# A fused linear-attention and mixture-of-adapters kernel on one core: a new hand-written order, earlier last loads, a longer gate ahead of the stores, head-by-head sums in the last two batches

## The chip, the cores and the metric

The kernel runs on one core of one Trainium2 chip. The metric is device microseconds of one execution. A core has TensorE (PE in the profile), VectorE (DVE), ScalarE (ACT), GpSimd (POOL) and SyncE (SP); each runs its own list of instructions strictly in order, and semaphores between them hold an instruction back until what it needs is there. Sixteen DMA engines move data between HBM and SBUF.

## The reference, cut to what matters

Shapes: q, k and v are (8 batches, 8 heads, 576 positions, 64), float32; the output is (4608, 512).

```python
def phi(x, c, s):                       # c, s: cos and sin of pi/2 * pos / 576
    r = np.maximum(x, 0.0)
    return np.concatenate([r * c, r * s], axis=-1)
q_p = phi(q, cos_w, sin_w); k_p = phi(k, cos_w, sin_w)
kv = np.einsum('bhsf,bhsd->bhfd', k_p, v)          # sums over positions
z  = np.sum(k_p, axis=2)
num = np.einsum('bhsf,bhfd->bhsd', q_p, kv)
den = np.einsum('bhsf,bhf->bhs', q_p, z)[..., None] + 1e-06
x = (num / den) -> rows of 8 heads * 64 = 512
logits = x @ w_gate                                 # 8 experts, the best 2 count
w = softmax of the best 2 logits
out = x + sum over the 2 experts of w * (x @ A[e]) @ B[e]   # rank 16
```

## The kernel before, in words

**Order.** Everything is unrolled. The text `ORDER` (line 21) is one list of jobs, written out by hand: a name, an engine letter (T TensorE, A ScalarE, V VectorE, G GpSimd, S SyncE; W is GpSimd too) and indices. The program issues the jobs in this order, so the order of a letter's jobs is the order of that engine's queue. A job marked W also waits until the last VectorE job of the kinds `vs`, `rk` or `qc` ahead of it in the list has ended (line 493, reason "port").

**Per batch b.** `ldv`, `ldk`, `ldq` (lines 199 to 210) load v, k and q, 1152 KB of float32 each, which all but the first v and k are turned into bf16 by the DMA on its way; these 22 loads are issued by GpSimd and land one after the other. `vs` (line 240) multiplies v by the cos or sin table: 18 jobs of 128x256 a batch, spread over ScalarE, VectorE and GpSimd. `rk` (line 246) is the relu of k, `qc` (line 277) that of q, in two halves of 128x1152. `kv` (line 253), in three parts, lets TensorE sum k times (v, 1) over the positions into the PSUM tile `big`. `kve` (line 271) copies the sums to SBUF as bf16, in two jobs of 64 partitions, each into its own block of a tile whose other blocks stay zero (`kz`, line 264, sets them once), so that one matmul serves two heads.

**Per step n.** The 4608 tokens are 36 steps of 128 tokens, 4.5 steps a batch; step 4 of each nine takes 64 tokens of two batches ("mixed"). In a step: `qt` (line 284) transposes q, `qe` (line 292, VectorE) multiplies by the cos and sin tables, `nd` (line 299) does the matmuls for numerators and denominators, `re` and `no` (lines 332, 335, VectorE) divide, `xt` (line 346) transposes x, `xe` (line 351) copies it out of PSUM, `za` (line 355) multiplies by A and w_gate, `mx` (line 361, VectorE) finds the best logits. From step 27 on (`ROWS`), but not in the mixed step 31, `nd` uses 64-row matmuls, one head each. In each `nd`, the k-th division of the trace (`xt<-nd`) is that of step k.

**Per group of three steps.** VectorE does `nm` (sum of the best two logits, line 366), `mk`, `tt`, `cb`, ScalarE `sg` (sigmoid), VectorE `zg`; TensorE `zt` and a copy `ze` turn the result. Then, per step, `dx` (line 427) adds x and the adapters' part in one of the PSUM banks b0 and b1 (the two halves of `big`, which `kv` also uses) or q0 and q1; `oe` (line 442) copies the result to an output tile (22 of them, most laid over the loads of the first batches), and `st` (line 446) stores it, 256 KB.

**Gate.** SyncE's queue holds the first loads, then `gate` (line 219), then the 36 stores. `gate` is two tiny DMAs: the first reads a word of the last v and so waits for its load, the second reads what the first wrote and so waits for that one to land. Every store is queued behind.

Of the kernel before, what the change touches and what calls it, by code (L numbers as in the profile page):

```python
# [15 lines left out]
HALF = 64  # L16
# [5 lines left out]
ldv,S,0,0 pre,G start,A ldk,S,0,0 ldw,S ldq,G,0,0 tq,A ldv,G,1,0 ldk,G,1,0 ldq,G,1,0 ldv,G,2,0 vs,A,0,3,0  # L22
vs,V,0,5,1 ldk,G,2,0 cols,V vs,A,0,4,1 vs,V,0,7,1 vs,A,0,5,0 kz,G,1 kz,V,2 vs,A,0,8,0 vs,A,0,8,1 vs,A,0,1,0
vs,V,0,4,0 vs,A,0,7,0 kz,V,0 vs,A,0,0,1 vs,A,0,2,1 vs,A,0,0,0 vs,V,0,6,0 vs,A,0,1,1 vs,A,0,3,1 rk,V,0,0 rk,A,0,1
vs,V,0,2,0 vs,V,0,6,1 kv,T,0,0 qc,V,0,1 kv,T,0,1 qc,V,0,0 kv,T,0,2 qt,T,1 kve,A,0,0 qt,T,0 kve,A,0,1 qe,V,0
cw,A,0 qe,V,1 dm,T,n0 dm,T,n0 dm,T,n0 nd,T,0 qt,T,3 re,V,0 qt,T,2 no,V,0 qe,V,3 vs,G,1,8,0 vs,A,1,3,1 dm,T,b0
dm,T,b0 nd,T,1 vs,A,1,5,0 vs,G,1,6,1 vs,V,1,2,0 xt,T,0 vs,A,1,6,0 vs,W,1,7,1 xe,A,0 re,V,1 qe,V,2 vs,G,1,5,1
vs,A,1,8,1 vs,G,1,0,1 no,V,1 vs,A,1,2,1 ldq,G,2,0 vs,A,1,4,1 vs,V,1,1,1 dm,T,b0 dm,T,b0 dm,T,b0 dm,T,b0 dm,T,b0
dm,T,b0 nd,T,2 vs,V,1,1,0 vs,A,1,0,0 rk,V,1,0 ldv,G,3,0 xt,T,1 vs,A,1,7,0 xe,A,1 vs,V,1,4,0 ldk,G,3,0 dm,T,b0
kv,T,1,0 vs,V,1,3,0 re,V,2 za,T,0 no,V,2 ldq,G,3,0 kv,T,1,1 mx,V,0 nd,T,3 qc,V,1,0 xt,T,2 kv,T,1,2 re,V,3  # L30
qc,V,1,1 xe,A,2 za,T,1 no,V,3 kve,A,1,1 qt,T,4 qt,T,5 kve,A,1,0 za,T,2 qe,V,4 xt,T,3 mx,V,1 xe,A,3 mx,V,2 nd,T,4
# [5 lines left out]
vs,A,2,8,1 qc,V,2,0 xt,T,6 mk,V,1 kv,T,2,1 nm,V,1 re,V,7 xe,A,6 tt,V,1 cb,V,1 no,V,7 kv,T,2,2 sg,A,1 qt,T,9
zg,V,1 kve,A,2,0 nd,T,8 vs,W,3,0,1 qe,V,9 kve,A,2,1 vs,G,3,0,0 xt,T,7 zt,T,1 qt,T,10 vs,G,3,5,0 re,V,8 za,T,6
ze,A,1 no,V,8 qt,T,11 vs,G,3,5,1 xe,A,7 dx,T,2,b0 qe,V,10 vs,G,3,1,1 nd,T,9 oe,A,2 vs,G,3,2,1 qe,V,11 xt,T,8
vs,A,3,2,0 vs,G,3,8,1 za,T,7 dx,T,3,b1 re,V,9 xe,A,8 ldq,G,5,0 mx,V,7 no,V,9 dx,T,4,b0 vs,A,3,1,0 za,T,8  # L40
rk,V,3,0 vs,G,3,6,1 nd,T,10 oe,A,4 oe,A,3 xt,T,9 mx,V,6 mx,V,8 qt,T,12 re,V,10 vs,W,3,4,1 nm,V,2 vs,A,3,3,0
# [12 lines left out]
zt,T,4 no,V,17 vs,G,5,7,1 za,T,15 dx,T,11,b0 xe,A,16 vs,G,5,3,0 mx,V,15 qe,V,19 nd,T,18 ze,A,4 vs,G,5,4,0
# [56 lines left out]
def kernel(ctx, tc, q, k, v, w_gate, A, Bw, out):  # L111
# [107 lines left out]
    def gate(e, b):  # L219

        e.dma_start(out=gone, in_=v_b[b][0:1, 0, 0, 0:2])
        e.dma_start(out=gone2, in_=gone)
# [301 lines left out]
```

## Time and profile before

| | |
|---|---|
| runs shown | 105.68, 105.83, 105.94 us; median 105.83 |
| profiled execution, whole | 105.92 us |
| its span (first to last thing recorded) | 104.1 us |
| TensorE clock granted | 0.997 |

The span is 1.8 us shorter than the execution's own time; what lies around it is taken to be the same for both kernels. Sections 1 and 2 of the profile tell how full each engine is and when; the chain of waits tells which work ended last; the timeline gives single instructions: start, duration, engine, line, output, input, and in brackets the idle time before it and what ended that.

### The profile page before, as it was taken

To read this page: it belongs to the slowest core of one execution; us is meant where nothing else is said; L and a number is where in the kernel's file an instruction comes from. 1 tells how busy PE (TensorE), PEld (TensorE's weight loads), DVE (VectorE), ACT (ScalarE), POOL (GpSimd) and SP (SyncE) were. 2 spreads that over 40 slices of the span, in tenths; PEclk is the share of its full clock that TensorE was granted. 3 is DMA by queue.
4 is the path that set the end of the run, shared out by engine and by line. 5 is a ranking of instruction groups with operands and counts; after the bars stand their busy time and mean duration, and the time that the engine had idled before them with its cause. 6 is when DMAs were issued, how large, how long until landed. Compare 5 with 4: busy or idle time off the path is not lost.

```text
span 104.1 us, 3984 instructions
## 1 busy us (share of the span) xinstructions
PE 91.0 (87%) x1620; PEld 65.7 (63%) x1620; DVE 87.3 (84%) x264; ACT 82.3 (79%) x176; POOL 57.3 (55%) x112
## 2 busy tenths in 40 slices
PE   4999489879794999999999999999999999998810
PEld 1344267457573887867887789688778677665200
DVE  5058769579995999999999999999999999999710
ACT  6969767918899699999899789979984896967820
POOL 6991004960799696997979869998910000000000
PEclk9999999999999999999999999999999999999998
DMA  2999999999999999999999999999999996989992
GB/s 27 364 358 291 216 208 247 208 207 213 203 208 213 204 206 210 208 213 204 208 210 205 208 207 207 210 206 126 188 397 372 349 334 257 376 307 383 381 384 96
DMA packets 19225, 25.55 MB, mean 245 GB/s; under 512 B 2184, under 2 KB 13448, under 8 KB 19208
## 3 DMA queue, kind: packets, MB, share of 16 engines
q0 software_dynamic: 11616, 12.98, 73.8%
q1 hardware_dynamic: 7064, 12.21, 32.8%
q8 instruction: 12, 0.20, 0.7%
q10 hardware_dynamic: 528, 0.13, 0.6%
q14 instruction: 5, 0.04, 0.1%
HBM read 28.85 MB, written 9.44 MB: 368 GB/s over the span
## 4 chain that ended last, share of the span: by engine, by line
PE 53%; DMA 18%; ACT 11%; POOL 9%; issue 2%; DVE 2%; POOLq 0%; ACTq 0%
DMA q<-in_q_dram 18%; PE nd L324 10%; PE big L258 8%; PE xz L349 6%; PE za L358 6%; PE big L439 6%; PE big L440 5%; PE pq L289 5%; POOL vs L244 4%; ACT xT L353 3%; ACT zgT L423 2%; PE nd L313 2%; POOL q L200 2%; PE xz L415 2%; POOL k L200 1%
## 5 line engine op out<-in xcount | busy, mean ns | idle before, releaser
L244 POOL TENSOR_SCALAR vs<-v,tab 128x256 bf16<-128x256 bf16 x78 | 37.9, 501 | 17.8 <-DMA v<-in_v_dram 8.7
L353 ACT COPY xT<-xz 128x512 bf16<-128x512 bf16 x34 | 20.0, 587 | 8.9 <-PE xz L349 8.3
L297 DVE TENSOR_TENSOR qT<-pq,tabq 128x1024 bf16<-128x1024 bf16 x36 | 23.8, 676 | 0.9 <-PE pq L289 0.8
L243 ACT ACTIVATE vs<-v,tab 128x256 bf16<-128x256 bf16 x43 | 20.0, 512 | 0.9 <-DMA v<-in_v_dram 0.6
L343 DVE TENSOR_TENSOR xt<-nd,rden 128x512 bf16<-128x512 f32 x28 | 19.2, 687 | 0.3
L324 PE MATMUL nd<-kvsb,qT 128*128 128x130 bf16 (+1 forms) x256 | 19.1, 221 | 0.4 <-DVE qT L297 0.4
L258 PE MATMUL big<-vs,k 64*64 64x130 bf16 x576 | 12.4, 221 | 4.3 <-DVE k L251 2.7
L324 PEld LDWEIGHTS <-qT 128*128 128x128 bf16 (+1 forms) x256 | 13.6, 100 | 2.9 <-issue 1.1
L349 PE MATMUL xz<-ident,xt 128*128 128x128 bf16 x144 | 14.1, 220 | 1.2 <-DVE xt L343 0.7
L358 PE MATMUL za<-AW,xT 128*128 128x136 bf16 x144 | 14.4, 223 | 0.1
L258 PEld LDWEIGHTS <-k 64*64 64x64 bf16 x576 | 9.2, 106 | 7.2 <-DVE k L251 3.5
L289 PE MATMUL pq<-ident,qq 128*128 128x128 bf16 x144 | 13.0, 219 | 0.2 <-DVE qq L282 0.2
L439 PE MATMUL big<-xt,turn 128*128 128x512 bf16 x31 | 11.7, 378 | 0.4 <-ACT k L444 0.3
L349 PEld LDWEIGHTS <-xt 128*128 128x128 bf16 x144 | 10.2, 114 | 2.6 <-DVE xt L343 0.9
L440 PE MATMUL big<-Ball,zgT 128*128 128x512 bf16 x31 | 11.8, 380 | 0.0
L468 PE MATMUL nd<-ones 128*128 128x512 bf16 x36 | 9.4, 427 | 1.5 <-DVE eps_hi L469 1.5
L275 ACT CAST kvsb<-big 64x520 bf16<-64x520 f32 x16 | 9.5, 593 | 1.5 <-PE big L258 1.1
L358 PEld LDWEIGHTS <-xT 128*128 128x128 bf16 x144 | 9.4, 98 | 1.9 <-ACT xT L353 0.8
L289 PEld LDWEIGHTS <-qq 128*128 128x128 bf16 x144 | 9.2, 98 | 1.9 <-DVE qq L282 0.3
L319 PE MATMUL nd<-eps_hi,ones 128*128 128x4 bf16 x56 | 9.5, 169 | 0.1
L282 DVE TENSOR_SCALAR qq<-q 128x1152 bf16<-128x1152 bf16 x16 | 8.1, 513 | 0.8 <-DMA q<-in_q_dram 0.8
L468 PEld LDWEIGHTS <-ones 128*128 128x128 bf16 x36 | 3.8, 108 | 6.6 <-issue 1.9
(81 smaller groups left out, 148.1 us busy)
## 6 DMA issues: line engine op xcount, KB each, us to landing
q<-in_q_dram POOLq DMA_DIRECT2D x8, 576.0 KB, 17.1
v<-in_v_dram POOLq DMA_DIRECT2D x7, 576.0 KB, 17.6
k<-in_k_dram POOLq DMA_DIRECT2D x7, 576.0 KB, 17.0
out_dram<-k SPq DMA_DIRECT2D x10, 256.0 KB, 4.2
out_dram<-v0f SPq DMA_DIRECT2D x8, 256.0 KB, 4.5
out_dram<-k0f SPq DMA_DIRECT2D x8, 256.0 KB, 3.8
out_dram<-v SPq DMA_DIRECT2D x6, 256.0 KB, 3.3
v0f<-in_v_dram SPq DMA_DIRECT2D x1, 1152.0 KB, 5.5
```

Of the source, the lines that this page charges most:

```text
L243: return e.activation(dst, src, AF.Copy, bias=0.0, scale=t)
L244: return e.tensor_scalar(out=dst, in0=src, scalar1=t, scalar2=1.0, op0=ALU.mult, op1=ALU.mult)
L258: e.matmul(out=big[halves[g2], par, gp * 2 * W:(gp + 1) * 2 * W], lhsT=k_b[b][pr, 2 * gp + g2, s, :], rhs=vs_t[b % NV][pr, s, 2 * gp + g2, ...
L289: e.transpose(out=d[:, gp, :, jj, :], in_=q2_t[b % 3][:, gp, s].rearrange("p g d -> p (g d)"), identity=ident)
L297: e.tensor_tensor(out=qT_t[n % NQ], in0=src, in1=tab, op=ALU.mult)
L324: e.matmul(out=nd[pr, par, gp * 2 * W:(gp + 1) * 2 * W], lhsT=qT[:, i, gp * 2 + par, js], rhs=kv_t[b % 3][:, par, gp, i, :], start=False, ...
L343: e.tensor_tensor(out=x.rearrange("p (a t d) -> p t a d", t=2, d=D), in0=nds()[:, :, :, 0:D], in1=rd.rearrange("p (t a) -> p t a", t=2).to ...
L349: e.transpose(out=xz[:, c * 128:(c + 1) * 128], in_=x[:, c], identity=ident)
L353: (e.copy if e is nc.scalar else e.tensor_copy)(xT_t[n % 3], src)
L358: e.matmul(out=zs[:, i, :], lhsT=xT_t[n % 3][:, c, :], rhs=AW[:, c, :], start=(c == 0 and i == 0), stop=(c == DCH - 1), skip_group_check=True)
L439: e.matmul(out=d, lhsT=turn, rhs=x_t[n % NX], start=True, stop=False)
L440: e.matmul(out=d, lhsT=zgT_t[g % 3][:, n - GROUPS[g][0], :], rhs=Ball, start=False, stop=True)
```

## The change: what it does

1. **Loads.** GpSimd issues the same 22 loads. Two more stand ahead of its first `vs`; the last v (batch 7) now goes ahead of the k of batch 6; and the last load of all, q of batch 7, stands behind the seventh GpSimd `vs` of batch 5, where it stood behind the second of batch 7.
2. **Gate and stores.** `gate` gets a third copy, which waits for the second to land. The stores stand nearly in the order of the steps (0, 1, 2, 4, 3, 6, 5, ...), where they stood mixed (1, 8, 7, 0, 2, 18, 3, 20, ...).
3. **Sums of batches 6 and 7, head by head.** `kve` of these copies all 128 partitions in one job into dense tiles, and the mixed step 31 uses 64x64 matmuls: 36 in place of 18. No zeros are needed there.
4. **Late q by GpSimd.** One half of q of batch 6 and both of batch 7 (`qc`) are done by GpSimd, and `nm` of four groups (6, 7, 8, 11) too.
5. **Order anew.** All the rest of `ORDER` is written anew. VectorE's share of `vs` in batch 0 goes from 6 to 11; from the first `qe` of step 4 on, VectorE loses 3 `qc`, 4 `nm`, 1 `oe` and 1 `mx` and gains 1 `ze`; GpSimd has 75 `vs`, where it had 78; ScalarE gains 3 `vs` and 1 `oe`, and loses 2 `kve`, 1 `cw` and 1 `ze`.

```diff
-ROWS = 27
+ROWS, DENSE = 27, True
+def dense(b):
+    return DENSE and b >= ROWS // 9 * 2
 def gate(e, b):
     e.dma_start(out=gone, in_=v_b[b][0:1, 0, 0, 0:2])
     e.dma_start(out=gone2, in_=gone)
+    e.dma_start(out=gone3, in_=gone2)
 def kve(e, b, g2):
+    copy = e.copy if e is nc.scalar else e.tensor_copy
+    if dense(b):
+        return copy(kv_t[b % 3][:, :, :, :, 0:W], big[:, :, 0:4 * W].rearrange("p t (y i w) -> p t y i w", y=2, i=2))
 def nd_(e, n):
+    if mixed(n) and dense(tok[0][0]):
+        jobs = [(g2, pr, js, kv_t[tok[j][0] % 3]) for g2, pr in enumerate(halves) for j, js in enumerate(halves)]
+        for g2, pr, js, _ in jobs:
+            e.matmul(out=nd[js, g2, D:4 * W:W], lhsT=ones[pr, 0:HALF], rhs=eps_hi2[pr], start=True, ...)
+        for gp in range(2):
+            for par in range(2):
+                for i in range(2):
+                    for g2, pr, js, kvb in jobs:
+                        a = gp * 2 + par
+                        e.matmul(out=nd[js, g2, a * W:(a + 1) * W], lhsT=qT[pr, i, a, js], rhs=kvb[pr, par, gp, i, 0:W], ...)
+        return
 def no(e, n):
-    if by_rows(n):
+    if by_rows(n) or dense(tokens(n)[0][0]):
 def nm(e, g):
+    if e is nc.gpsimd:
+        m8 = m8_t[g % 2]
+        return e.tensor_tensor(out=ms_t[g % 2][:, 0:n], in0=m8[:, 0:n, 0], in1=m8[:, 0:n, 1], op=ALU.add)
```

GpSimd's queue from the last loads on, before and after (of `vs` the batch, position and table):

```
before: ... ldk5 ldv6 ldk6 vsW,4,6,1 ldv7 ... ldq6 ... vsW,5,6,1 ldk7 ... vs,7,4,0 vs,7,1,1 ldq7 vsW,7,7,1 vs,7,4,1 vsW,7,0,0
        vs,7,7,0 vs,7,3,0 vs,7,3,1 vsW,7,5,1 vs,7,6,0 vs,7,8,0
after:  ... ldk5 vs,3,8,1 ldv6 ... ldv7 ldk6 ... ldq6 ... ldk7 ... ldq7 ... vs,6,0,0 vs,7,1,1 vs,7,6,0 vs,7,7,1 nm6 vsW,6,7,0
        vs,7,6,1 vs,7,5,1 vs,6,6,0 vs,7,2,1 qc6,1 vsW,7,2,0 vs,7,0,0 nm7 vsW,7,3,0 vs,7,1,0 qc7,0 qc7,1 nm8 nm11
```

VectorE's queue, before and after, from step 21 to step 27 (the step, group or batch behind the name):

```
before: re21 mx19 mx18 no21 rk6 mx20 qe24 mk6 nm6 re22 tt6 no22 cb6 qe25 zg6 re23 qc6,0 no23 qc6,1 qe26 re24 mx22 no24 rk7
        qe27 re25 mx21 mx23 no25 mk7 nm7 qe28 tt7 re26 cb7 no26 zg7 qc7,1 re27 no27 qc7,0
after:  re21 no21 mx19 qe24 mx20 rk6 mk6 re22 tt6 cb6 no22 zg6 qe25 re23 no23 qe26 qc6,0 re24 mx21 no24 mx22 rk7
        qe27 re25 mx23 no25 mk7 qe28 tt7 re26 cb7 no26 zg7 qe29 re27 no27
```

More of the change, by code (lines that the diff above doesn't have):

```diff
@@ L21 @@
 ORDER = """
[L22 to L31, printed above, removed]
@@ L37 @@
[L37 to L41, printed above, removed]
@@ new lines @@
+xe,A,22 qe,V,26 nd,T,24 kve,A,6,0 qc,V,6,0 za,T,22 vs,W,7,2,0 xt,T,23 re,V,24 dx,T,17,b0 mx,V,21 no,V,24
+vs,G,7,0,0 xe,A,23 dx,T,18,b1 gate,S,7 st,S,0 vs,A,7,4,0 mx,V,22 rk,V,7,0 qt,T,27 za,T,23 oe,A,18 st,S,1 nd,T,25
+qe,V,27 oe,A,17 st,S,2 xt,T,24 qt,T,28 vs,A,7,0,1 re,V,25 mx,V,23 dx,T,20,b1 no,V,25 st,S,4 xe,A,24 nm,G,7
+vs,W,7,3,0 dx,T,19,b0 vs,A,7,8,1 mk,V,7 st,S,3 qe,V,28 vs,G,7,1,0 nd,T,26 oe,A,20 qc,G,7,0 st,S,6 qt,T,29 tt,V,7
+oe,A,19 qt,T,30 re,V,26 cb,V,7 xt,T,25 no,V,26 sg,A,7 kv,T,7,0 vs,A,7,4,1 zg,V,7 st,S,5 xe,A,25 nd,T,27 qe,V,29
@@ L271, in kve @@
     def kve(e, b, g2):
+        copy = e.copy if e is nc.scalar else e.tensor_copy
+        if dense(b):
+            return copy(kv_t[b % 3][:, :, :, :, 0:W], big[:, :, 0:4 * W].rearrange("p t (y i w) -> p t y i w", y=2, i=2))
         src = big[halves[g2], :, 0:4 * W].rearrange("p t (y i w) -> p t y i w", y=2, i=2)
         dst = kv_t[b % 3][halves[g2], :, :, :, g2 * W:(g2 + 1) * W]
-        (e.copy if e is nc.scalar else e.tensor_copy)(dst, src)
+        copy(dst, src)
     def qc(e, b, h):
```

115 lines of the change are left out of this document (65 added, 50 removed).

## The prediction

> **What bounds the kernel now.** I read the page's busy times first, then the windows, the waits, and last the timeline around single stalls.
>
> ```profile
> PE 91.0 (87%) x1620; PEld 65.7 (63%) x1620; DVE 87.3 (84%) x264; ACT 82.3 (79%) x176; POOL 57.3 (55%) x112
> HBM read 28.85 MB, written 9.44 MB: 368 GB/s over the span
> ```
>
> Four engines over half full, so no average settles it. The windows (start:end, length, then busy us of PE, PEld, DVE, ACT, POOL, clock, share of the DMA engines, GB/s) do:
>
> ```profile
> 30.00:35.00 5.00, 3.61 (x97) 3.16 (x99) 3.77 (x14) 3.89 (x10) 4.21 (x7) 1.00 1.22 210
> 60.00:65.00 5.00, 4.96 (x132) 4.30 (x131) 4.93 (x16) 4.49 (x11) 4.26 (x10) 1.00 1.22 209
> 70.00:75.00 5.00, 5.00 (x89) 4.08 (x87) 5.00 (x15) 4.71 (x11) 4.56 (x8) 1.00 1.05 152
> 75.00:80.00 5.00, 4.87 (x127) 3.86 (x126) 4.96 (x17) 3.68 (x9) 0.94 (x3) 1.00 1.06 378
> ```
>
> From 60 to 65 and from 70 to 80 VectorE is busy 4.93 to 5.00 of every 5 us, and TensorE nearly so; ScalarE follows until 75. Of these only 30 to 35 shows a hole in VectorE (3.77). So VectorE's work sets the pace, and an instruction taken off it is worth its time wherever nothing else is late first. What can be late first are the loads, which land one after another. From the chain of waits, the second q load, fourth of GpSimd's 22, was issued at 4.85 and took 18.72, so it landed at 23.57; SyncE's first gate copy, which waits for the last v load (19th), went out at 66.37:
>
> ```profile
> 4.85 18.72 DMA q<-in_q_dram
> 66.37 0.75 SPq L221 DMA_DIRECT2D gone<-v  x1
> 70.85 0.58 SPq L222 DMA_DIRECT2D gone<-gone  x1
> 71.55 0.67 SPq L451 DMA_DIRECT2D out_dram<-v0f  x1
> 69.91 0.79 POOL L200 DMA_DIRECT2D q<-in_q_dram  x1
> ```
>
> That is (66.37 - 23.57)/15 = 2.85 us a load: the 18th at 63.5, the 19th at 66.4, the 20th at 69.2, the 21st at 72.1, the 22nd at 74.9 if it is issued in time. In before it isn't: it goes out at 69.91, and the DMA engines run partly empty (152 GB/s from 70 to 75).
>
> The end: the last output copy on ScalarE ends at 99.38 + 0.58 = 99.96, and the stores flow at full rate on to 102 and a little further (0.16 of the engines in the microsecond behind).
>
> ```profile
> 99.38 0.58 ACT v L444
> 76.00:78.00 2.00, 1.87 (x62) 1.63 (x59) 2.00 (x7) 1.65 (x5) 0.00 (x0) 1.00 1.06 406
> 92.00:102.00 10.00, 6.40 (x62) 3.32 (x59) 6.26 (x21) 6.12 (x14) 0.00 (x0) 1.00 1.03 383
> 85.00:88.00 3.00, 3.00 (x60) 2.24 (x59) 2.81 (x12) 2.15 (x5) 0.00 (x0) 1.00 0.63 234
> 102.00:103.00 1.00, 0.00 (x0) 0.00 (x0) 0.00 (x0) 0.00 (x0) 0.00 (x0) 1.00 0.16 59
> ```
>
> So two limits meet at 102.2: the compute chain, and the stores, which had a hole (234 GB/s from 85 to 88) and were still draining a queue after it.
>
> **The change part by part. Early stretch.** Batches 0 and 1 wait for loads whose places in the queue don't change (the first 17 keep theirs), so until step 4 I count nothing: more `vs` for VectorE fall into its waits there. Between 30 and 35 one stall stands out:
>
> ```profile
> 31.47 0.79 POOL L200 DMA_DIRECT2D q<-in_q_dram  x1
> 32.30 1.20 POOL L244 TENSOR_SCALAR vs<-v,tab 128x256 bf16<-128x256 bf16 x2
> 33.10 0.31 PE L258 MATMUL big<-vs,k 64*64 64x130 bf16 x8 [1.22 <-POOL vs L244]
> 33.90 0.17 DVE L364 MAX8 m<-za 128x8 f32<-128x8 f32 x1 [1.20 <-PE za L358]
> ```
>
> The first sums of batch 2 wait 1.22 us for a GpSimd `vs`, queued behind a load; VectorE then waits 1.20. In the new order all GpSimd `vs` that this part of `kv` needs stand ahead of those loads, so the stall should go. Between nothing and 1.2 us is gained; what of it reaches the end is capped by the next item.
>
> **Loads.** The k of batch 6 becomes the 19th load: 66.4 in place of 63.5. `rk` of batch 6 cannot start before it.
>
> ```profile
> 66.11 0.80 DVE L251 TENSOR_SCALAR k<-k 128x2304 bf16<-128x2304 bf16 x1
> 67.66 0.17 DVE L380 TENSOR_TENSOR mk<-za,m 128x24 f32<-128x24 f32 x1
> 73.28 0.96 DVE L251 TENSOR_SCALAR k<-k 128x2304 bf16<-128x2304 bf16 x1
> ```
>
> Before, `rk6` (66.11), `mx20` and `qe24` are done when `mk6` starts at 67.66. The new order has the other two ahead of `rk6`, so `mk6` can start at 66.4 + 0.8 = 67.2: **at most 0.5 us ahead here**, however much was gained earlier. I take the whole 0.5, since the gain of 1.2 covers it; the low end is 0. `rk7` may start from 72.1, against 73.28: a cap of 1.2 there.
>
> **Late q on GpSimd.** VectorE's starts tell what is freed: from each to the next start, the four halves of batches 6 and 7 cost 0.71, 0.37, 0.41 and 0.37 us (the first while GpSimd issued its last load).
>
> ```profile
> 70.05 0.21 DVE L333 RECIPROCAL rden<-nd 128x8 f32<-128x8 f32 x1
> 70.17 0.79 DVE L282 TENSOR_SCALAR qq<-q 128x1152 bf16<-128x1152 bf16 x1
> 70.88 0.67 DVE L343 TENSOR_TENSOR xt<-nd,rden 128x512 bf16<-128x512 f32 x1
> 71.48 0.45 DVE L282 TENSOR_SCALAR qq<-q 128x1152 bf16<-128x1152 bf16 x1
> 71.85 0.67 DVE L297 TENSOR_TENSOR qT<-pq,tabq 128x1024 bf16<-128x1024 bf16 x1
> 77.78 0.45 DVE L282 TENSOR_SCALAR qq<-q 128x1152 bf16<-128x1152 bf16 x1
> 78.19 0.21 DVE L333 RECIPROCAL rden<-nd 128x8 f32<-128x8 f32 x1
> 79.03 0.45 DVE L282 TENSOR_SCALAR qq<-q 128x1152 bf16<-128x1152 bf16 x1
> 79.40 0.24 DVE L364 MAX8 m<-za 128x8 f32<-128x8 f32 x2
> 67.75 0.15 DVE L373 TENSOR_REDUCE ms<-m 128x3 f32<-128x6 f32 x1
> 67.81 0.20 DVE L333 RECIPROCAL rden<-nd 128x8 f32<-128x8 f32 x1
> ```
>
> Gone up to `rk7`: one half of batch 6 (0.39, about the cheaper one) and `nm6` (0.06) = 0.45; behind it both halves of batch 7 (0.41 + 0.37) and `nm7`, 0.06, together 0.84, hidden by nothing on VectorE, which is full there (4.96 of 5). Of the tail's two `oe` on VectorE one goes, the last, which had only ScalarE's own last copy behind it, and `ze12` comes in: nothing.
>
> What it costs on GpSimd is not in this trace. The nearest rows:
>
> ```profile
> L244 POOL TENSOR_SCALAR vs<-v,tab x78: 467/473/1061, 16.9 to 75.5; 128x256 bf16<-128x256 bf16 x78
> masks.py:199 POOL TENSOR_SCALAR_AFFINE_SELECT ident<-ident x1: 292/292/292, 1.5 to 1.5; 128x128 bf16<-128x128 bf16 x1
> L282 DVE TENSOR_SCALAR qq<-q x16: 406/460/785, 13.0 to 79.0; 128x1152 bf16<-128x1152 bf16 x16
> ```
>
> By proportion to a `vs`: 4.5 x 0.473 = 2.13 us; by the slope between the 128 and the 256 columns, 0.473 + 896 x 1.41 ns = 1.74. I estimate 1.9, between them. Behind `rk6` (done at 67.2) GpSimd has nine `vs` (4.3 us) and three halves (5.7), so 77.2 without waiting; but q7 lands at 74.9, so 74.9 + 3.8 = **78.7**. TensorE needs it for `qt31`, which before started at 82.02:
>
> ```profile
> 82.02 0.39 PE L289 MATMUL pq<-ident,qq 128*128 128x128 bf16 x4
> ```
>
> Up to 82.02 - 78.7 = 3.3 us of gain, then, GpSimd isn't late. But these long jobs can hold up VectorE. Its relu took 460 ns as a rule and 785 at most: the extra 0.33 us is below one `vs` of 0.473, as if each waits for the other's running instruction. GpSimd's first half can start at 69.6 (q6 at 69.2; five `vs` of 0.473 behind `rk6`) and ends at 71.5. VectorE had `re23` at 70.05; 0.5 earlier and with `no23` (0.60 to the next start) and `qe26` (0.67 at most) ahead of it, its own half of batch 6 comes at about 70.9. So I count **a wait of 0.6** (71.5 less 70.9); it is 0 if there is no such coupling, 2.1 if GpSimd starts just ahead of VectorE. The Trainium skill (SBUF — State Buffer, "SBUF: two separate sides") says that GpSimd and a VectorE instruction in a two-port mode share a port pair under an exclusive lock, held for the whole instruction; the rows agree as far as they go, since no wait is longer than one `vs`. By this rule the wait is as counted, and without it the sum would be 0.6 lower. Speaking against my 1.9 us is the skill's GPSIMD Engine Reference, 3.1: a simple body runs at 1.03 cycles an element, which makes about 1.0 us and some overhead for 1152 at 1.2 GHz, an estimate; by it there would be no wait and the sum would be 103.9. No row shows such a job.
>
> **Sums head by head.**
>
> ```profile
> L275 ACT CAST kvsb<-big 64x520 bf16<-64x520 f32 x16 | 9.5, 593 | 1.5 <-PE big L258 1.1
> 77.23 0.54 PE L258 MATMUL big<-vs,k 64*64 64x130 bf16 x24
> ```
>
> One `kve` of 128 partitions in place of two of 64 saves ScalarE one copy (0.59) a batch; it also gets three more `vs` there, so nothing. Step 31 has 18 matmuls more, each of half the columns: between nothing and 18 x 0.54/24 = 0.4 us, the price of twice as wide ones in `kv`; I take nothing, since TensorE is the less full engine by then (4.87 against 4.96).
>
> **Gate and stores.** The last v is now the 18th load: 63.5. The first copy took 70.85 - 66.37 = 4.5 us to let the second go; two such waits give 63.5 + 9.0 = 72.5, and the third copy 0.6: first store at **73.1**, against 71.55. The loads are out by then or soon (the last lands at 74.9, before it would have run past 76). In before the first stores flowed at full rate only from 76, behind the loads; now from about 75: 9.44 MB at 383 GB/s take 24.6 us, so 99.6 if nothing holds them, against 102.2 or so. In order of steps no store waits for a late copy until the last ten, so the hole from 85 to 88 goes, and with it the queue at the end, worth up to 0.5 us; I take 0.2.
>
> **Sum.** 105.92 - 0.5 - 0.45 - 0.84 + 0.6 - 0.2 = 104.5. The median of the runs shown lies 0.09 below the profiled execution; I make no correction: **104.5 us**.
>
> **The rivals.**
>
> *Slower: GpSimd's long relus hold VectorE.* If GpSimd reaches its half of batch 6 only when VectorE comes to its own (1.4 us later than worked out, as when `rk6` or q6 is late), VectorE waits the full 2.1; the 0.5 is then not there either. 105.92 - 0.45 - 0.84 + 2.1 = 106.7. For it: 785 ns against 460 once a relu met GpSimd; GpSimd gets 4.3 us more work (5.7 less three `vs`) in its fullest stretch (4.56 of 5 from 70 to 75). Against: `vsW` jobs wait for VectorE, so only this one pair can meet. It decides from a wait of 1.6 us on.
>
> *No difference: nothing but VectorE gets freer.* TensorE (4.96 of 5) and ScalarE (4.71) are as full until 75; if they hold the pace, and the new order makes as many stalls as it removes, only the 0.2 at the end stays: 105.7.
>
> *The stores are the bound.* If the first store lands as late after its issue as before (at full rate from 76 or 77 on), the last ends at 76.5 + 24.6 = 101.1 against 102.2: no better than 104.8, whatever compute does.
>
> *The tail shrinks too.* The 0.5 in full, no wait for GpSimd, 0.5 at the end: 105.92 - 0.5 - 0.45 - 0.84 - 0.5 = 103.6; earlier than the stores allow (99.6 for 102.2, so 103.3) it can't be.
>
> **How the numbers follow.** What a measurement can tell from no change is about 0.3%, here 105.5 to 106.15. Forecast, 103.9 to 105.1: 0.50. Tail shrinks: 0.12. Stores bound, 104.8 to 105.4: 0.10. No difference: 0.11. Slower: 0.17. So faster 0.72, same 0.11, slower 0.17. The range runs from 103.2 (tail case, 0.4 lower for its bounds) to 106.6 (into the slower case).
>
> **What would show it.** Right: no stall of about 1.2 us in VectorE's rows at 32; `rk6` starting at 66.4 behind a DMA wait or just after; first store issued near 73; last load issued near 57 and landed at 75; 380 GB/s without a hole from 76 on; GpSimd relus of 1.9 us and one VectorE relu of about 1 us near 71; the last copy ending at 98.5. Wrong: TensorE waiting for `qq` at `qt31`, new holes in VectorE between 35 and 65, or a store queue still draining long after the last copy.

## The result, and the profile after

The changed kernel took 110.20, 110.78 and 111.81 us, beside 105.68 to 106.20 of the kernel before on the same chip: **1.047 times as long, 95% interval 1.037 to 1.058**. The forecast was 104.5 and a range up to 106.6. A fourth run, in a disturbed state of the chip, is left out of the ratio, as such runs are below, while a time given ahead of a ratio is the median of all its runs. The profiled execution is the one of 110.20, with a span of 108.3 and a granted clock of 0.998.

Busy time and traffic, from the page of the changed kernel:

```profile
PE 91.5 (84%) x1636; PEld 65.1 (60%) x1636; DVE 91.0 (84%) x262; ACT 80.0 (74%) x170; POOL 67.2 (62%) x118
HBM read 28.85 MB, written 9.44 MB: 353 GB/s over the span
```

VectorE was to have less to do, and is busy 3.7 us longer (91.0 for 87.3) with two instructions fewer. Of these, 1.5 us are the five more `vs` of batch 0. The relus of q and k alone take 15.4 us for 13.8, though there are three fewer: one of q takes 710 ns on average for 513, one of k 911 for 812. So instructions got longer: it waits inside them. GpSimd has 9.9 us more (67.2 for 57.3). The windows show where (columns as before):

```profile
30.00:35.00 5.00, 4.93 (x120) 3.81 (x117) 5.00 (x16) 4.45 (x11) 4.50 (x7) 1.00 1.21 207
60.00:65.00 5.00, 3.89 (x115) 3.31 (x113) 4.93 (x14) 4.00 (x10) 3.78 (x9) 1.00 1.21 208
70.00:75.00 5.00, 4.89 (x111) 3.66 (x99) 4.93 (x9) 4.18 (x10) 5.00 (x6) 1.00 1.05 195
75.00:80.00 5.00, 3.88 (x52) 3.09 (x53) 5.00 (x16) 3.69 (x10) 3.15 (x7) 1.00 0.96 358
85.00:88.00 3.00, 2.62 (x54) 1.78 (x55) 2.08 (x6) 1.71 (x4) 0.49 (x2) 1.00 1.02 376
92.00:102.00 10.00, 9.22 (x127) 5.72 (x125) 9.10 (x31) 7.61 (x17) 0.20 (x1) 1.00 0.54 200
```

From 30 to 35 VectorE has no hole any more (5.00 for 3.77). From 70 to 75 it is as busy as before with 9 instructions in place of 15. From 92 to 102 the DMA engines run at half (200 GB/s for 383): the stores wait for results that come late.

GpSimd's timeline from 62 on tells why:

```profile
62.79 6.90 POOL L250 TENSOR_SCALAR vs<-v,tab 128x256 bf16<-128x256 bf16 x14 [1.22 <-DVE qq L291]
69.66 0.19 POOL L399 TENSOR_TENSOR ms<-m 128x3 f32<-128x3 f32 x1
69.84 2.30 POOL L250 TENSOR_SCALAR vs<-v,tab 128x256 bf16<-128x256 bf16 x5
72.11 3.13 POOL L291 TENSOR_SCALAR qq<-q 128x1152 bf16<-128x1152 bf16 x1
75.64 0.94 POOL L250 TENSOR_SCALAR vs<-v,tab 128x256 bf16<-128x256 bf16 x2 [0.41 <-DVE qq L291]
78.02 0.20 POOL L399 TENSOR_TENSOR ms<-m 128x3 f32<-128x3 f32 x1 [1.44 <-DVE m L388]
78.19 0.94 POOL L250 TENSOR_SCALAR vs<-v,tab 128x256 bf16<-128x256 bf16 x2
79.10 6.22 POOL L291 TENSOR_SCALAR qq<-q 128x1152 bf16<-128x1152 bf16 x2
```

A half of q takes GpSimd 3.12 us, and it comes to the last two at 79.10, behind a wait for VectorE's relu (a `vsW` job) and one of 1.44 for `nm7`. VectorE's own instructions, from its timeline (the relu of k5, its half of q of batch 6, `qe` of step 31):

```profile
60.38 1.80 DVE L257 TENSOR_SCALAR k<-k 128x2304 bf16<-128x2304 bf16 x1
73.30 2.24 DVE L291 TENSOR_SCALAR qq<-q 128x1152 bf16<-128x1152 bf16 x1
85.64 0.69 DVE L306 TENSOR_TENSOR qT<-pq,tabq 128x1024 bf16<-128x1024 bf16 x1 [1.54 <-PE pq L298]
```

Its half of batch 6 takes 2.24 us where 0.45 is the rule: it ends at 75.54, 0.30 behind the end of GpSimd's (72.11 + 3.13 = 75.24). The relu of k5 takes 1.80, where before it took 0.74:

```profile
59.78 0.74 DVE L251 TENSOR_SCALAR k<-k 128x2304 bf16<-128x2304 bf16 x1
```

And at step 31 VectorE waits 1.54 us for TensorE, which waits for GpSimd:

```profile
85.38 0.23 PE L298 MATMUL pq<-ident,qq 128*128 128x128 bf16 x1 [1.67 <-POOL qq L291]
103.50 0.59 ACT L471 COPY v<-pq 128x512 f32<-128x512 f32 x1 [0.31 <-PE pq L467]
```

The last output copy ends at 104.09, 4.1 later than before, and the span with it. The start of VectorE's division of some steps, from the traces of the two kernels and of five experiments below, shows where the time goes ("late q back" has VectorE do the late q, "quick op" a quick GpSimd form of it, "two meetings" late q back and two meetings at the port away, "three pieces" the GpSimd relu in pieces, "best" the fastest version):

```
step   before  after   late q back  quick op  two meetings  three pieces  best
 3     24.42   24.90   24.81        24.96     24.20         25.19         24.52
 7     35.01   34.62   34.53        34.68     34.46         34.91         35.00
18     59.19   59.11   58.98        59.11     58.16         59.54         59.17
19     61.48   62.98   62.85        62.98     61.13         63.42         61.58
22     68.05   70.20   70.05        70.18     69.04         70.64         68.09
24     72.67   75.69   74.24        73.91     73.29         74.67         72.50
28     80.44   83.11   82.31        81.46     81.35         82.04         80.12
29     82.12   86.57   84.14        83.28     83.17         86.89         82.05
35     93.96   98.08   95.56        94.70     94.75         99.51         93.62
```

After is level with before at step 18 and loses 1.6 at step 19 (k5), 0.65 more by step 22, 0.9 more by step 24 (q of batch 6) and 1.8 at step 29 (q of batch 7). The last row of "three pieces" can't be compared: behind its step 29 the trace has TensorE's clock at half for a while (below).

### The profile page after: what moved, and what is told of

Its sections match the earlier page's. It is cut to its first block, busy times and chain, and to the rows that moved or that the text cites. A ratio compares the mean times of both kernels' runs of the same rounds, so it can differ in the third digit from the quotient of the medians.

```text
span 108.3 us, 4032 instructions
## 1 busy us (share of the span) xinstructions
PE 91.5 (84%) x1636; PEld 65.1 (60%) x1636; DVE 91.0 (84%) x262; ACT 80.0 (74%) x170; POOL 67.2 (62%) x118
## 4 chain that ended last, share of the span: by engine, by line
DVE 34%; PE 20%; DMA 17%; POOL 17%; issue 4%; ACT 4%; POOLq 0%; ACTq 0%
DMA q<-in_q_dram 17%; DVE xt L367 9%; DVE qT L306 8%; POOL vs L250 7%; DVE qq L291 7%; POOL qq L291 6%; PE xz L373 3%; PE big L466 3%; DVE k L257 3%; PE big L467 3%; DVE zg L436 2%; PE za L382 2%; PE pq L298 2%; DVE rden L357 2%; PE nd L348 1%
## 5 line engine op out<-in xcount | busy, mean ns | idle before, releaser
L250 POOL TENSOR_SCALAR vs<-v,tab 128x256 bf16<-128x256 bf16 x75 | 35.8, 495 | 14.4 <-DMA v<-in_v_dram 9.3
L377 ACT COPY xT<-xz 128x512 bf16<-128x512 bf16 x33 | 19.5, 590 | 6.6 <-PE xz L373 6.1
L249 ACT ACTIVATE vs<-v,tab 128x256 bf16<-128x256 bf16 x46 | 21.8, 518 | 1.3 <-DVE ms L400 1.1
L367 DVE TENSOR_TENSOR xt<-nd,rden 128x512 bf16<-128x512 f32 x27 | 18.6, 688 | 0.3
L348 PE MATMUL nd<-kvsb,qT 128*128 128x130 bf16 (+1 forms) x240 | 18.3, 221 | 0.2 <-DVE qT L306 0.2
L298 PE MATMUL pq<-ident,qq 128*128 128x128 bf16 x144 | 13.5, 220 | 3.1 <-POOL qq L291 1.7
L348 PEld LDWEIGHTS <-qT 128*128 128x128 bf16 (+1 forms) x240 | 13.1, 99 | 2.6 <-issue 1.7
L284 ACT CAST kvsb<-big 64x520 bf16<-64x520 f32 x12 | 7.1, 593 | 4.4 <-PE big L264 4.3
L399 POOL TENSOR_TENSOR ms<-m 128x3 f32<-128x3 f32 (+1 forms) x4 | 0.8, 196 | 15.0 <-DVE m L388 15.0
L291 POOL TENSOR_SCALAR qq<-q 128x1152 bf16<-128x1152 bf16 x3 | 9.3, 3123 | 0.0
```

Of the source, the lines that this page charges most:

```text
L249: return e.activation(dst, src, AF.Copy, bias=0.0, scale=t)
L250: return e.tensor_scalar(out=dst, in0=src, scalar1=t, scalar2=1.0, op0=ALU.mult, op1=ALU.mult)
L291: return e.tensor_scalar(out=dst, in0=src, scalar1=0.0, scalar2=None, op0=ALU.max)
L298: e.transpose(out=d[:, gp, :, jj, :], in_=q2_t[b % 3][:, gp, s].rearrange("p g d -> p (g d)"), identity=ident)
L348: e.matmul(out=nd[pr, par, gp * 2 * W:(gp + 1) * 2 * W], lhsT=qT[:, i, gp * 2 + par, js], rhs=kv_t[b % 3][:, par, gp, i, :], start=False, ...
L367: e.tensor_tensor(out=x.rearrange("p (a t d) -> p t a d", t=2, d=D), in0=nds()[:, :, :, 0:D], in1=rd.rearrange("p (t a) -> p t a", t=2).to ...
```

## The experiments: GpSimd's late q

The theory: GpSimd's relus are the cause, through two waits (VectorE's for the port at batch 6, TensorE's for the result of batch 7). The rival: the new order is the cause, and the relus stand where some other wait would.

**Late q back to VectorE, the rest as changed.**

```diff
-qc,G,6,1 ... qc,G,7,0 ... qc,G,7,1
+qc,V,6,1 ... qc,V,7,0 ... qc,V,7,1
```

> The changed kernel with the three late halves of q (batch 6 half 1, batch 7 halves 0 and 1) done by VectorE again, at the same places of the list; the four nm stay with GpSimd. Theory A, GpSimd's relu is the cause (3.12 us each in the changed kernel's trace): VectorE's relu of batch 6 is 0.45 us again and not 2.24 (1.8 back), TensorE no longer waits 1.67 at step 31, VectorE pays 3 x 0.4 = 1.2 us for the three relus. Net 2.3 faster than the changed kernel, about 107.9 beside its profiled 110.2, ratio to the kernel before about 1.02. Rival B, the new order costs the time and the relus only stand where some other wait would: the same as the changed kernel within 0.5 us, ratio 1.04 to 1.05.

107.63 us, ratio 1.013 (1.007 to 1.018). So the three relus cost 1.047 - 1.013 = 3.4%, about 3.6 us, more than the 2.3 expected. The rival is not dead: 1.3% stays.

**The same three halves by GpSimd, in the kernel before.**

```diff
-qc,V,6,1 ... qc,V,7,1 ... qc,V,7,0
+qc,G,6,1 ... qc,G,7,1 ... qc,G,7,0
```

> The kernel before with one edit: the same three halves of q by GpSimd, at their places in the old list. Theory A: GpSimd's relus take 3.1 us each here too; the one of batch 6 meets two-port instructions of VectorE, and the two of batch 7 (its q lands at 76.6) end at 76.6 + 6.2 = 82.8 or later, behind the 82.0 at which TensorE wants them; VectorE is spared 1.2 us. Between 106 and 109 us, slower than before. Rival B, the relus are harmless or help: 104.7 to 105.9.

110.40 us, ratio 1.041 (1.033 to 1.049), above the range expected. From its timeline (line numbers of before):

```profile
71.67 3.13 POOL L282 TENSOR_SCALAR qq<-q 128x1152 bf16<-128x1152 bf16 x1
72.79 2.62 DVE L251 TENSOR_SCALAR k<-k 128x2304 bf16<-128x2304 bf16 x1
74.86 0.28 PE L289 MATMUL pq<-ident,qq 128*128 128x128 bf16 x2 [1.60 <-POOL qq L282]
84.73 0.34 PE L289 MATMUL pq<-ident,qq 128*128 128x128 bf16 x3 [2.33 <-POOL qq L282]
```

The victim is another (the relu of k7, 2.62 us), the kinds of wait are the same. So the edit alone, without the new order, makes most of the loss.

**What sets 3.12 us.** GpSimd's halves as two multiplies:

```diff
+        if e is nc.gpsimd:
+            return e.tensor_scalar(out=dst, in0=src, scalar1=1.0, scalar2=1.0, op0=ALU.mult, op1=ALU.mult)
```

> The changed kernel with GpSimd's three halves of q as x * 1.0 * 1.0 in place of max(x, 0): this leaves out the relu on those halves. It measures what sets 3.12 us. If it is the operation (max is dearer on GpSimd than the two multiplies of a vs, which take 0.473 us for 256 columns), each takes about 4.5 x 0.473 = 2.1 us and the kernel is some 2 us faster. If it is the size or shape (1152 columns in one instruction), each takes 3.1 us again and the time is unchanged.

The group of GpSimd's q in this kernel (busy, mean ns of one):

```profile
L292 POOL TENSOR_SCALAR qq<-q 128x1152 bf16<-128x1152 bf16 x3 | 3.4, 1148 | 0.0
```

1.15 us, far below the 2.1 expected for the operation: the shape isn't the cause. The kernel took 107.47 us (a single execution). Then three forms, one for each half:

```diff
+            if (b, h) == (6, 1):
+                return e.tensor_scalar(out=dst, in0=src, scalar1=1.0, scalar2=None, op0=ALU.mult)
+            ops = (ALU.max, ALU.mult) if h == 0 else (ALU.mult, ALU.max)
+            return e.tensor_scalar(out=dst, in0=src, scalar1=0.0 if h == 0 else 1.0,
+                                   scalar2=1.0 if h == 0 else 0.0, op0=ops[0], op1=ops[1])
```

> The changed kernel with a different form of instruction for each of GpSimd's three halves of q: batch 6 half 1 as x * 1.0 with one operation (no relu there), batch 7 half 0 as max(x, 0) * 1.0, batch 7 half 1 as max(x * 1.0, 0). The two multiplies took 1.15 us, max alone 3.12 us. Theory A, the operation max is the dear one: 1.15, 3.1 or more, 3.1 or more; time then about 108.5 to 110. Theory B, the form with one operation is the dear one: 3.1, 1.15, 1.15; time then about 109.

```profile
L295 POOL TENSOR_SCALAR qq<-q 128x1152 bf16<-128x1152 bf16 x2 | 8.2, 4108 | 0.0
L293 POOL TENSOR_SCALAR qq<-q 128x1152 bf16<-128x1152 bf16 x1 | 3.1, 3132 | 0.0
```

Both theories fall. A single multiply takes 3.13, like max; max with a multiply, in either order, 4.11; two multiplies 1.15. So on this GpSimd the pair multiply-multiply is a quick form and every other one tried is slow. A `vs` is such a pair: that is why its row priced the relu wrongly. (A single execution: 114.31 us.)

**The relu in three pieces of 384 columns.**

```diff
+        if e is nc.gpsimd:
+            for s in range(0, NS, 3):
+                done = e.tensor_scalar(out=dst[:, :, s:s + 3, :], in0=src[:, :, s:s + 3, :], ...)
+            return done
```

> The changed kernel with each of GpSimd's three late halves of q as three instructions of 384 columns in place of one of 1152. GpSimd's work stays (three times about 1.05 us). Theory A, the port is handed over between instructions: VectorE's relu of batch 6 waits at most one piece, 0.45 + 1.05 = 1.5 us at most against 2.24, and the kernel gains 0.5 to 1.0; TensorE's wait at step 31 stays. Rival B, VectorE does not get the port between pieces that follow each other without a pause (as at the relu of k5, which was held over two boundaries): the relu takes 2.2 us or more again, and the time is unchanged.

110.99 us, ratio 1.042 (1.036 to 1.049): no gain that can be told from the changed kernel. VectorE's relu (first row) and TensorE's step 31 (second), from the timeline, and GpSimd's group:

```profile
73.75 0.78 DVE L295 TENSOR_SCALAR qq<-q 128x1152 bf16<-128x1152 bf16 x1
85.31 0.29 PE L302 MATMUL pq<-ident,qq 128*128 128x128 bf16 x1 [2.63 <-POOL qq L293]
```

```profile
L293 POOL TENSOR_SCALAR qq<-q 128x384 bf16<-128x384 bf16 x9 | 10.7, 1214 | 0.0
```

VectorE's relu is short (0.78 for 2.24), as theory A has it, and VectorE is 1.0 us earlier at step 24. That the port is handed over at the end of a piece isn't shown: VectorE came at 73.75, just where the second piece begins (73.71), and was done at 74.53, while that piece, by its record, runs to 74.88 and the third takes 1.61 us for 1.16. And all of the gain is given back at step 29, where TensorE's wait grows from 1.67 to 2.63: GpSimd ends q of batch 7 at 85.3 either way. So in the changed kernel the time behind step 29 is set by GpSimd's queue, and whatever VectorE gains ahead of it is lost. In this profiled execution TensorE's clock was granted at half just behind that (the column ahead of the last two); in that stretch it falls from 0.32 us behind the changed kernel (step 29) to 1.43 behind (step 30, 89.71 for 88.28), and there it still is at step 35:

```profile
86.00:88.00 2.00, 2.00 (x27) 1.36 (x27) 1.78 (x6) 0.78 (x2) 0.00 (x0) 0.50 1.04 380
```

**Another engine.** In a version of the old order (early q7, two copies in the gate, dense sums; below), both halves of batch 7 go to ScalarE.

```diff
-qc,V,7,1 ... qc,V,7,0
+qc,A,7,1 ... qc,A,7,0
```

> The kernel of the run before (early q7, two copies, head-by-head sums, old order) with both halves of q of batch 7 by ScalarE. Theory A, the idea of taking late q off VectorE is sound and GpSimd was the wrong engine: ScalarE needs about 1.1 us a half (an estimate from 0.51 us for 256 columns), has that much idle time from 77 to 83, and the kernel gains a further 0.2 to 0.6 us: ratio 0.990 to 0.995. Rival B, VectorE's freed time is worth nothing there, since TensorE is as full, or ScalarE's copies of x come late behind the relus: the same as without it or 0.3 to 1 slower.

107.47 us, ratio 1.012 (1.008 to 1.017), 0.5 slower than without it (106.93; the intervals just overlap), and compute is 1.0 later at step 35 (94.40 for 93.42). ScalarE takes 1.20 us a half, nearly as estimated, and its copies come late behind them. From ScalarE's and TensorE's timeline:

```profile
79.31 1.17 ACT L290 ACTIVATE qq<-q 128x1152 bf16<-128x1152 bf16 x1
80.37 0.58 ACT L450 COPY zgT<-xz 128x384 bf16<-128x384 bf16 x1
81.00 0.38 PE L373 MATMUL xz<-ident,xt 128*128 128x128 bf16 x4 [0.85 <-ACT zgT L450]
```

So the idea doesn't pay on this engine either. With the quick GpSimd form too, the relief of VectorE by 1.2 us brought compute only 0.86 us (94.70 against 95.56 at step 35, beside the late q back), and the time 0.1, which can't be told from none (107.47 against 107.59, one profiled execution of each). In both, the DMA engines still write at 291 and 369 GB/s from 103 to 104, some 2 us after the last output copy has ended (100.69 and 101.56): the stores end both kernels, and the gain in compute doesn't reach the time.

## The experiments: meetings at the shared port

**The relu of k5.** Three `vs` follow each other on GpSimd while it waits. One of them is moved behind it:

```diff
-vs,G,5,2,0 oe,A,13 za,T,17 rk,V,5,0
+oe,A,13 za,T,17 rk,V,5,0 vs,W,5,2,0
```

> The changed kernel with one GpSimd vs (batch 5, position 2, table 0) moved from just ahead of VectorE's relu of k of batch 5 to just behind it, where it waits for that relu's end. Theory A, the run of three GpSimd vs back to back held that relu for two instruction boundaries: the relu takes 0.75 to 1.0 us and not 1.80, and the kernel is 0.8 to 1.0 us faster than the changed kernel. Rival B, the 1.06 us are made up elsewhere (ScalarE, loads): no difference beyond 0.3 us in time, though the relu is short.

110.88 us, ratio 1.042 (1.035 to 1.049); the changed kernel's 1.047 lies inside. From its VectorE timeline:

```profile
60.32 0.90 DVE L257 TENSOR_SCALAR k<-k 128x2304 bf16<-128x2304 bf16 x1
...
68.08 1.44 DVE L257 TENSOR_SCALAR k<-k 128x2304 bf16<-128x2304 bf16 x1
```

The relu is short, and 0.97 is gained at step 19 (62.01 for 62.98). But 0.61 of it is gone at step 20 (64.60 for 64.96), and that is the edit's own price: the moved `vs` now waits for the relu, the sums of batch 5 on TensorE wait for that `vs`, and VectorE for TensorE.

```profile
62.12 1.33 PE L264 MATMUL big<-vs,k 64*64 64x130 bf16 x56 [0.43 <-POOL vs L250]
64.36 0.21 DVE L357 RECIPROCAL rden<-nd 128x8 f32<-128x8 f32 x1 [0.51 <-PE nd L348]
```

In the changed kernel these sums wait for the relu of k alone. By step 22 the gain is 0.27, since the relu of k6 now meets a run of `vs` (1.44 for 0.77), and at step 29 GpSimd sets the time again. So rival B holds in the changed kernel.

**Late q back, and two meetings taken away** (k5 as above, and the zeroing of GpSimd, `kz,G,1`, which met q of batch 1, into a wait for loads):

```diff
-xe,V,2 kz,G,1 kv,T,1,1
+xe,V,2 kv,T,1,1
-ldv,G,3,0 vs,V,0,7,0
+ldv,G,3,0 kz,G,1 vs,V,0,7,0
```

> The changed kernel with the three late halves of q back on VectorE, one GpSimd vs of batch 5 moved behind VectorE's relu of k5, and GpSimd's zeroing of the tile of batch 1 (kz) moved from the middle of batch 1 to the wait behind its eighth load. Theory A, what stays of the loss with the late q back (1.0129 to the kernel before, 1.4 us) is mostly VectorE's two-port instructions meeting GpSimd's work in the new order (1.06 us at the relu of k5, 0.5 us at q of batch 1): 1.2 us faster than with the late q back alone, ratio 1.000 to 1.005. Rival B, the meetings only take the place of other waits: 107.3 to 107.7 us, ratio 1.011 to 1.014.

106.78 us, ratio 1.0055 (1.002 to 1.009). With GpSimd no longer the last, the meetings count: 0.85 us off, of the 1.2 expected, and the ratio comes out at the upper edge of theory A. (The intervals of the two ratios overlap a little; at step 35 the traces differ by 0.81.) Of what k5 gave, step 20 again takes 0.6, by the same wait of VectorE for TensorE (0.51), and k6 another 0.24:

```profile
59.44 0.89 DVE L257 TENSOR_SCALAR k<-k 128x2304 bf16<-128x2304 bf16 x1
...
67.20 1.43 DVE L257 TENSOR_SCALAR k<-k 128x2304 bf16<-128x2304 bf16 x1
```

**That meeting away as well, and `nm` back on VectorE.**

```diff
-vs,G,7,7,1 ... rk,V,6,0 nm,G,6 oe,A,16 vs,W,6,7,0 ... nm,G,7 ... nm,G,8 ... nm,G,11
+rk,V,6,0 nm,V,6 oe,A,16 vs,W,7,7,1 vs,G,6,7,0 ... nm,V,7 ... nm,V,8 ... nm,V,11
```

> The changed kernel with the late q and the four nm back on VectorE and with three meetings taken away: those at q of batch 1 and k of batch 5 as in the run with two (ratio 1.0055), and one more GpSimd vs moved behind VectorE's relu of k6, which there took 1.43 us against 0.80 before. Theory A, what is left of the loss is that meeting (0.6) and the wait for nm6 on GpSimd: ratio 0.998 to 1.002, 105.7 to 106.2. Rival B, what is left lies in the stores and the longer gate: ratio 1.004 to 1.006 again.

106.80 us, ratio 1.005 (1.002 to 1.008): nothing gained. The relu of k6 is short (0.98), but in this profiled execution the first loads came later (relu of k1 at 21.03 for 20.61), and it ends where the one before did. The wait at step 20 is still there (0.52). What is left, 0.5%, is not in the meeting at k6.

## The experiments: loads, gate, stores, dense sums

**The kernel before with the early last load and the third copy.**

```diff
-ldq,G,7,0 xt,T,22
+xt,T,22
-dx,T,13,b0 ldk,G,7,0
+dx,T,13,b0 ldk,G,7,0 ldq,G,7,0
+    e.dma_start(out=gone3, in_=gone2)
```

> The kernel before with two edits of the loads and the gate alone: the last load (q of batch 7) is issued right behind k of batch 7, and the gate has its third copy; the order of stores is the old one. Theory A, the DMA part of the change is sound: the last load is issued near 57 and lands at 75, the first store goes out at about 75, and the time is within 0.5 us of before (105.4 to 106.1). Rival B, the longer gate costs: the stores end later by the 2 us or so by which the first goes out later, 106.5 to 108.

106.22 us, ratio 1.003 (1.001 to 1.005). **With the early last load and two copies:**

> The kernel before with one edit: the last load (q of batch 7) is issued right behind k of batch 7; the gate keeps its two copies. With the third copy as well the ratio was 1.003, its first store went out at 74.87, and the DMA engines were nearly empty from 74 to 76 (0.15 of the stretch). Theory A, the third copy opened that hole: with two copies the first store goes out near 71.4, no hole, and the time is 105.2 to 105.9 (ratio 0.995 to 1.000). Rival B, the early load itself costs, since stores and the last load then share the DMA engines: ratio 1.002 to 1.006 again.

106.10 us, ratio 0.9975 (0.995 to 1.0005). One stretch of each, the third copy first (the last two columns are the share of the DMA engines and GB/s):

```profile
74.00:76.00 2.00, 2.00 (x26) 1.43 (x24) 1.84 (x8) 2.00 (x6) 1.42 (x4) 1.00 0.15 24
```

```profile
74.00:76.00 2.00, 2.00 (x27) 1.44 (x24) 1.84 (x8) 2.00 (x6) 1.39 (x4) 1.00 1.01 349
```

In the old order, where v of batch 7 is the 19th load, the third copy lets the loads run dry before the first store (74.87). In the new order it is the other way. **The run with three meetings away, without the third copy:**

```diff
-    e.dma_start(out=gone3, in_=gone2)
```

> The changed kernel with the late q and nm on VectorE, three meetings taken away (ratio 1.0051), and the gate's third copy gone. Theory A, the new order of compute holds the 0.5% that is left: first store near 69, time unchanged within 0.2 us, ratio 1.004 to 1.006. Rival B, the longer gate holds it: ratio 0.999 to 1.002.

107.75 us, ratio 1.013 (1.009 to 1.018): both theories fall, for the third copy is worth 0.8% here. The first store goes out at 68.97, when three loads are still to land, and VectorE waits for q of batch 7:

```profile
77.69 0.46 DVE L290 TENSOR_SCALAR qq<-q 128x1152 bf16<-128x1152 bf16 x1 [0.52 <-DMA q<-in_q_dram]
```

That load landed at 77.6 there (issued at 56.93, 20.7 us), against 75.0 in the changed kernel (57.32, 17.7 us).

**All parts but the late q and the new order** (early q7, third copy, dense sums with one `kve`, stores in the order of the steps):

> The kernel before with all parts of the change but two: the old list stays except for its loads, gate and stores (q7 issued behind k7, third copy, stores in the order of the steps as their copies end), and the sums of batches 6 and 7 are head by head with one copy each; VectorE keeps all of q and nm. Theory A, these parts are sound and small: ScalarE has 1.2 us less to do, and the time is 0.3 to 0.8 us under before, 105.2 to 105.7. Rival B, they cost (the 36 matmuls of step 31, stores waiting in turn): 106.3 to 107.5.

107.76 us, ratio 1.014 (1.009 to 1.020), slower than either theory had it, though compute was 0.4 ahead of before at step 35. **The same with two copies and the old order of stores:**

> The kernel before with the early q7 and the head-by-head sums of batches 6 and 7 (one copy each, 36 matmuls in step 31), two copies in the gate, the old order of everything else, the stores too. With the early q7 alone the ratio was 0.9975. Theory A, these parts of the change are sound: compute ends 0.3 to 0.4 earlier (as it did with the third copy and stores in order of steps, where the stores then ended late), ratio 0.993 to 0.998. Rival B, they are what is left of the loss: ratio 1.003 to 1.008.

106.93 us, ratio 1.005 (1.002 to 1.009): compute is 0.54 ahead at step 35, and the time is longer. **The same with the stores in the order of the steps:**

```diff
-gate,S,7 st,S,1 rk,V,7,0 ... st,S,8 ... st,S,7 ... st,S,0 ... st,S,2
+gate,S,7 st,S,0 st,S,1 st,S,2 st,S,4 st,S,3 st,S,6 ...
```

> The kernel before with early q7, two copies in the gate, the head-by-head sums, and the stores in the order in which the steps' copies end; the rest of the old order. With the old order of stores the last copy ended at 99.42 (99.96 before), but a hole in the stores from 84 to 88 left the last store behind: 1.0054. Theory A, the hole was the cause: with stores in order it goes, the last store follows the last copy at once, ratio 0.993 to 0.998. Rival B, the early stores still run out of finished steps, or the DMA engines' rate sets the end: ratio 1.002 to 1.006.

**105.86 us, ratio 0.9953 (0.992 to 0.998): ahead of both kernels.** Windows of the mixed stores (first fence) and of the ordered ones (second):

```profile
84.00:88.00 4.00, 3.78 (x87) 2.59 (x85) 3.93 (x15) 3.20 (x8) 0.00 (x0) 1.00 0.52 194
92.00:102.00 10.00, 5.85 (x59) 3.07 (x57) 5.73 (x20) 5.57 (x13) 0.00 (x0) 1.00 0.97 362
```

```profile
84.00:88.00 4.00, 3.80 (x90) 2.71 (x88) 3.93 (x14) 3.23 (x8) 0.00 (x0) 1.00 0.90 333
92.00:102.00 10.00, 6.05 (x60) 3.15 (x58) 5.92 (x20) 5.76 (x14) 0.00 (x0) 1.00 0.76 284
```

The hole from 84 to 88 (194 GB/s) is gone (333), and behind 92 the DMA engines have room (0.76 for 0.97): the stores no longer bound the end, so the 0.3 us by which compute is earlier come through. (The profiled execution, 105.97, is one of the longer of its twelve runs, 105.36 to 106.31.)

This kernel differs from the one with all parts (ratio 1.014) by the gate's third copy alone. So with ordered stores and dense sums the third copy cost 1.9% in the old order, more than in the pair above (1.003 against 0.9975). Its hole ahead of the first store (74.87 for 71.65):

```profile
74.00:76.00 2.00, 2.00 (x28) 1.52 (x27) 2.00 (x9) 2.00 (x6) 1.79 (x4) 1.00 0.20 32
```

**The order of stores alone, without the dense sums:**

> The same without the head-by-head sums: the kernel before with early q7, two copies and stores in order. Early q7 alone gave 0.9975, with compute unchanged. Theory A, the order of stores is worth what the hole cost, but compute ends as before (99.96), so no more than 0.2 us: ratio 0.995 to 0.999. Rival B, the order of stores itself costs: above 1.002.

106.08 us, ratio 0.999 (0.996 to 1.002): no difference, as theory A has it. Together the two runs point to the dense sums as the source of the 0.5%, once the stores let it through, though their intervals overlap.

## Why the prediction was wrong, point by point

**The step that failed: "Late q on GpSimd", its price.** "I estimate 1.9, between them", bounded at 2.13 above by proportion to a `vs`. Measured: 3.12. The sign of being wrong that the prediction named came with it: TensorE waits 1.67 us for `qq` at `qt31`. The rows it was scaled from were of another form, a multiply pair, and the form decides (1.15, 3.13, 4.11 us for the same shape). Both bounds lie below it. The Trainium skill (GPSIMD Engine Reference, 3.1) gives 1.03 cycles an element for a simple body, about 1.0 us by the prediction's estimate; the multiply pair's 1.15 agrees, max and the single multiply don't.

**The second step that failed: what the new order costs.** The sum has no term for stalls that the new order adds. A right price alone would not have saved the forecast: with the quick form, which takes 1.15 us (and leaves out the relu), the kernel took 107.47 (a single execution), still longer than before. Of the 5.7 us by which the profiled 110.20 misses 104.5, then, 2.7 hang on the price and 3.0 on the rest: the meetings below, a gain in compute that the stores at the end swallow, and a part that stays open.

**"Up to 82.02 - 78.7 = 3.3 us of gain, then, GpSimd isn't late."** It ended at 85.3, 6.6 later. Of that 2.4 are the price (6.22 for 3.8), and 4.2 that it began at 79.10 and not at 74.9. Its queue was summed up as if it waited for nothing: 67.2, nine `vs` and one relu, so 73.4, and 74.9 for the load. But GpSimd came to this part of its list 2.5 late (69.66 for 67.2), for its run of 14 `vs` began behind a wait of 1.22 for VectorE's relu; the first long relu took 1.2 more than counted; and it waited 0.41 for VectorE's relu in a `vsW` job and 1.44 for VectorE's `mx` in `nm7`. What stood behind such waiting jobs on GpSimd was not followed.

**"A wait of 0.6", "only this one pair can meet".** The wait was 1.8 (2.24 less 0.45), as in the slower rival (up to 2.1); that mechanism was right. But it was not the only pair: `vs` met k5 (1.06 us), zeroing met q of batch 1 (0.5 at step 3), and others followed as soon as one was taken away. The rule that `vsW` jobs wait for VectorE was read as covering every `vs`; it covers only those marked. The lock for a whole instruction, cited from the Trainium skill (SBUF — State Buffer, "SBUF: two separate sides"), agrees with the long relu: VectorE's 2.24 us end 0.30 behind GpSimd's instruction. The pieces fit it less well: there VectorE was done before the second piece's record ends. At k5, "no wait is longer than one `vs`" did not hold. VectorE came at 60.38 and was done at 62.18; less its usual 0.74 it ran from about 61.4 on (an estimate), about where this run ended:

```profile
59.73 1.83 POOL L250 TENSOR_SCALAR vs<-v,tab 128x256 bf16<-128x256 bf16 x4
```

It ends at 61.56, 1.2 us after VectorE came: at two ends of a `vs` in between (about 60.65 and 61.1, an estimate from 1.83/4 us each) GpSimd's next one had the port first.

**The gain of 0.84 and 0.45 on VectorE.** With the relus quick and harmless, compute gained 0.86 of 1.2, and the time no more than 0.1, since the stores ended later than compute. So even for the idea itself the time came out nearer to the "no difference" rival than to the forecast, though not for its reason, a full TensorE or ScalarE.

**Right.** The stall of 1.2 us near 32 is gone: after is 0.56 behind at step 6 and 0.39 ahead at step 7. It didn't last: a new hole in VectorE, named as a sign of being wrong, stands at 38.4 (0.58 us for TensorE's `nd`), and after is 1.1 behind at step 10 (41.93 for 40.82) before it is level again at step 18. The gate and the loads came as worked out (1st row GpSimd, the others SyncE):

```profile
57.32 0.79 POOL L205 DMA_DIRECT2D q<-in_q_dram  x1
```

```profile
68.23 0.60 SPq L227 DMA_DIRECT2D gone<-gone  x1
72.69 0.55 SPq L228 DMA_DIRECT2D gone<-gone  x1
73.34 2.33 SPq L478 DMA_DIRECT2D out_dram<-v0f  x3
```

First store 73.34 (73.1 predicted), last load landed at 75.0 (74.9). The head-by-head sums cost nothing (32 matmuls of step 31 in 0.42 us). The cap at `rk6` (66.4) never decided, since compute was already late: `rk6` ran at 68.58.

**The end.** "In order of steps no store waits for a late copy": right in the old order, where it took the hole away, but worth something only together with the dense sums and with two copies in the gate.

**What stays open.** With late q on VectorE and the meetings away, the new order is still 0.5% slower. Its trace (three meetings away) is 0.97 us behind before at step 35, and 0.61 of that arose at step 20 (0.32 behind at step 19, 0.93 at step 20), by the wait for the `vs` that the experiment itself had moved. So part of what is left is the experiment's own. The gate is not the cause, since its third copy is worth 0.8% in that order; the dense sums seem to gain in the old order, but were not taken out of the new one. Whether the rest lies in the order of compute, of the loads or of the stores was not settled.

## What to carry to other kernels

Don't price an operation on GpSimd by the size of another operation: the same shape took 1.15, 3.13 or 4.11 us by its form alone, so without a row of that very form the range must be wide enough to change the sign. When work moves to an engine with its own queue of waits, work out when that engine comes to it, with each wait ahead of it, and who stands behind the result. A gate or an order of transfers is right only for one order of compute: the third copy cost 0.5 to 1.9% in one and saved 0.8% in the other, and a compute gain came through only when the stores had no hole. And look at what an edit of the order delays: the `vs` moved out of VectorE's way made TensorE wait one step later, which took back 0.6 of 0.97 us.

## What the runs showed of the hardware

- GpSimd's tensor_scalar on 128x1152 bf16: multiply-multiply 1.15 us, one operation (max or multiply) 3.12 to 3.13, max with multiply 4.11. In pieces of 384 columns max took 1.16 (the median), so each column cost about (3.12 - 1.16)/768 = 2.6 ns.
- VectorE does not always get the shared port at the end of the GpSimd instruction that it met: in a run of `vs` without a pause it waited over two ends (1.06 us at k5). Among pieces of 1.16 us without a pause, where it came just as one ended, its relu took 0.78 us.
- ScalarE's relu of the same half took 1.20 us.
